# Taking a D-skip off TensorE: x loaded into the output tile, multiplied by D and added on VectorE

## The chip, the cores and the metric

The kernel runs on one core of one Trainium2 chip. The metric is the device time of one launch in microseconds (us). The time before is 201.72 us, the median of three runs (201.47 to 202.68). A faster kernel is one whose time is over 2% lower.

A core has five engines that matter here. TensorE multiplies matrices into PSUM. VectorE and ScalarE move results from PSUM to SBUF and do elementwise work. GpSimd does some elementwise work, and SyncE issues most transfers. In this kernel each engine gets its instructions in the order of one fixed list. The DMA engines move data beside them. "Span" is the time from the first to the last instruction in the trace, and the device time is some 2 to 3 us longer. "Granted clock" is the share of full speed that TensorE was given.

## The reference, cut to what matters

Two halves with 640 columns each are computed and put side by side.

```python
def _A_ref(x, Lambda_re, Lambda_im, B_re, B_im, C_re, C_im, log_dt, Dskip):   # x: [1, 2048, 640]
    ...
    Bu = jnp.einsum("bld,pd->blp", x + 0j, B_bar)
    for t in range(L):
        h = Lam_bar[None, :] * h + Bu[:, t, :]
    ...
    y = 2.0 * jnp.einsum("blp,dp->bld", hseq, Cmat).real + x * Dskip[None, None, :]   # the D-skip
    return y

def _B_ref(q, k, v, shift_k, ssm_k, ssm_D):    # the other half: a short convolution, kv = k_shift * v,
    ...                                        # then a long convolution by FFT, times q
```

The change is about the term `x * Dskip`: one multiply and one add for each of 2048 x 640 outputs.

## The kernel before

The state-space half first multiplies x by B (40 "B products" of ten matmuls each). It then builds up states with "coefficient products" of small matrices M that are computed on chip, scans, and works down again. The last step is 16 output tiles of 128 x 640. Each tile is made in two half tiles. The D-skip is three more matmuls per half tile, x transposed times a diagonal matrix of D, accumulated into the same PSUM:

```python
def a_proj(self, r, i, due):
    ...
    for part in range(2):
        def f(e, part=part):
            ...
            for j in range(10):
                nc.tensor.matmul(P[:, part, 0:320], lhsT=hap(j), rhs=self.CT[:, j, c0:c0 + 320], start=(j == 0), stop=False)
            pieces = [(k, max(c0, 128 * k), min(c0 + 320, 128 * k + 128)) for k in range(5)]
            ...
            for q, (k, lo, hi) in enumerate(pieces):
                nc.tensor.matmul(P[:, part, lo - c0:hi - c0], lhsT=self.xT[:, k, i // 2, r, ...],
                                 rhs=self.diagD[:, k, lo - 128 * k:hi - 128 * k], start=False, stop=(q == len(pieces) - 1))
        op(f"py{part}_{r}{i}", ...)
    self.evac(f"ey_{r}{i}", 640, ...)          # PSUM to the output tile yo, on ScalarE (12) or VectorE (4)
    ...
    op(f"st_{r}{i}", ...)                      # the store
```

All engines get their instructions from one list of names, in which a letter picks the engine where there is a choice (A ScalarE, D VectorE, G GpSimd, S SyncE, numbers are buffers). A fragment:

```
... py0_21@0,1 e2h30/A e2h33/D kvs4/S e321/A py1_21 s2k23@2 ey_21/A s2h32@6 e2k23/D st_21/S ...
```

Here `e2h33/D` says that an evacuation of 1024 columns stands on VectorE at that place of its queue. The order is fixed before the run. An engine whose next instruction isn't ready waits for it, as TensorE does for 1.8 us at L909 in the waits below.

## Time and profile before

| before | value |
|---|---|
| time, span, granted clock (profiled run) | 202.26 us, 200.5 us, 1.000 |
| VectorE busy from 104 to 182 us | 67.8 of 78 us (87%) |
| TensorE idle behind the first 12 us, all waits listed | 3.8 us |
| first B product, first coefficient product, first projection | 11.9, 19.9, 104.6 us |
| last instruction of TensorE ends | 196.8 us |

The slices, the windows, the chain and the groups are shown in the prediction.

To follow TensorE I also matched its program with the trace and priced each block of matmuls with its undisturbed duration in the trace (a B product 1.077 us, a half tile 1.357 us and 0.143 us for its diagonals, and so on). The **lag** is the time at which a block starts minus the work done until then. It counts waits and slow stretches alike. Before, it is 9.9 us at the first coefficient product, 17.6 us at the first projection and 23.7 us at the end. The work is 196.8 - 23.7 = 173.1 us.

### The profile page before, as it was taken

To read this page: it belongs to the slowest core of one execution; us is meant where nothing else is said; L and a number is where in the kernel's file an instruction comes from. 1 tells how busy PE (TensorE), PEld (TensorE's weight loads), DVE (VectorE), ACT (ScalarE), POOL (GpSimd) and SP (SyncE) were. 2 spreads that over 40 slices of the span, in tenths; PEclk is the share of its full clock that TensorE was granted. 3 is DMA by queue.
4 is the path that set the end of the run, shared out by engine and by line. 5 is a ranking of instruction groups with operands and counts; after the bars stand their busy time and mean duration, and the time that the engine had idled before them with its cause. 6 is when DMAs were issued, how large, how long until landed. Compare 5 with 4: busy or idle time off the path is not lost.

```text
span 200.5 us, 8859 instructions
## 1 busy us (share of the span) xinstructions
PE 185.7 (93%) x4043; PEld 136.3 (68%) x4043; DVE 168.1 (84%) x264; ACT 148.1 (74%) x175; POOL 20.6 (10%) x35
## 2 busy tenths in 40 slices
PE   0599999979999999699999999999999999999982
PEld 0465566747777678467657777676787878788771
DVE  7899899876899999949988899788959999877540
ACT  4979998978899888389986749896967679752011
POOL 8056500700000000000000000100000010001010
PEclk9999999999999999999999999999999999999999
DMA  5999997999999999969995068509334334998985
GB/s 167 239 152 132 231 180 167 245 159 210 219 180 171 167 217 206 247 153 215 210 196 133 5 152 252 134 22 189 89 147 103 96 80 105 170 234 160 229 226 140
DMA packets 109959, 33.74 MB, mean 168 GB/s; under 512 B 107106, under 2 KB 108642, under 8 KB 109922
## 3 DMA queue, kind: packets, MB, share of 16 engines
q1 hardware_dynamic: 109668, 32.52, 83.9%
q8 instruction: 31, 0.51, 1.1%
q0 software_dynamic: 224, 0.66, 0.9%
q14 instruction: 6, 0.05, 0.1%
q10 hardware_dynamic: 30, 0.00, 0.0%
HBM read 9.19 MB, written 7.86 MB: 85 GB/s over the span
## 4 chain that ended last, share of the span: by engine, by line
PE 72%; DMA 14%; DVE 6%; ACT 3%; SPq 2%; issue 1%; POOL 0%; DVEq 0%; POOLq 0%; ACTq 0%
PE ps L806 20%; PE ps L658 17%; PE ps L909 9%; PE ps L945 8%; PE ps L231 4%; DMA s<-s 4%; PE ps L1001 4%; DMA s<-in_B_v_dram 4%; PE ps L233 4%; PE ps L1037 3%; DMA s<-in_A_x_dram 3%; DMA s<-in_B_ssm_k_dram 3%; DVE s L239 2%; PE ps L810 2%; ACT s L237 2%
## 5 line engine op out<-in xcount | busy, mean ns | idle before, releaser
L237 ACT CAST s<-ps 128x1024 bf16<-128x1024 f32 x86 | 84.1, 1018 | 16.9 <-PE ps L945 6.4
L658 PE MATMUL ps<-xT,BC 128*64 128x512 bf16 x400 | 49.1, 383 | 0.1
L806 PE MATMUL ps<-BC,hb 128*128 128x320 bf16 x240 | 36.4, 300 | 0.0
L658 PEld LDWEIGHTS <-BC 128*64 128x64 bf16 x400 | 22.3, 110 | 15.1 <-issue 0.9
L806 PEld LDWEIGHTS <-hb 128*128 128x128 bf16 x240 | 21.9, 98 | 8.7 <-issue 0.3
L968 DVE TENSOR_TENSOR s<-s,s 128x2048 bf16<-128x2048 bf16 x20 | 24.4, 1222 | 2.0 <-ACT s L237 0.7
L909 PE MATMUL ps<-R,s 64*64 64x128 bf16 x1280 | 22.5, 218 | 2.9 <-POOL s L831 1.8
L237 ACT CAST yo<-ps 128x640 bf16<-128x640 f32 x12 | 8.4, 698 | 22.7 <-PE ps L810 18.5
L909 PEld LDWEIGHTS <-s 64*64 64x64 bf16 x1280 | 18.7, 107 | 8.1 <-issue 3.7
L239 DVE CAST s<-ps 128x1024 bf16<-128x1024 f32 x14 | 17.0, 1220 | 8.3 <-PE ps L909 2.7
L945 PE MATMUL ps<-s,Wre 128*64 128x128 bf16 x320 | 21.4, 221 | 0.0
L763 DVE TENSOR_TENSOR hb<-ps,hb 128x512 bf16<-128x512 f32 x30 | 19.1, 684 | 2.8 <-PE ps L231 1.6
L945 PE MATMUL ps<-s,Wim 128*64 128x128 bf16 x320 | 21.2, 219 | 0.0
L945 PEld LDWEIGHTS <-Wre 128*64 128x64 bf16 x320 | 18.2, 110 | 2.5 <-issue 0.5
L884 DVE TENSOR_TENSOR s<-s,s 128x2048 bf16<-128x2048 bf16 x15 | 18.3, 1222 | 1.0 <-ACT s L876 0.7
L945 PEld LDWEIGHTS <-Wim 128*64 128x64 bf16 x320 | 18.1, 110 | 1.1
L1044 DVE TENSOR_TENSOR s<-ps,s 128x1024 bf16<-128x1024 f32 x10 | 11.8, 1216 | 4.1 <-PE ps L1037 3.9
L237 ACT CAST hb<-ps 128x768 bf16<-128x768 f32 x17 | 13.7, 808 | 1.1 <-PE ps L658 1.1
L968 DVE TENSOR_TENSOR s<-s 128x1024 bf16<-128x1024 bf16 x20 | 13.8, 688 | 0.3
L231 PE MATMUL ps<-hb,M 128*64 128x256 bf16 (+1 forms) x136 | 13.3, 296 | 0.0
L1037 PE MATMUL ps<-Ct,s 128*64 128x64 bf16 x640 | 11.6, 196 | 0.8 <-DMA s<-s 0.7
L1037 PEld LDWEIGHTS <-s 128*64 128x64 bf16 x640 | 11.1, 113 | 1.9 <-DMA s<-s 0.9
(157 smaller groups left out, 261.4 us busy)
## 6 DMA issues: line engine op xcount, KB each, us to landing
s<-in_B_ssm_k_dram SPq DMA_DIRECT2D x5, 512.0 KB, 4.7
kvd<-s SPq DMA_DIRECT2D x5, 512.0 KB, 4.4
s<-kvd SPq DMA_DIRECT2D x5, 512.0 KB, 5.6
s<-in_B_q_dram SPq DMA_DIRECT2D x5, 512.0 KB, 4.4
out_dram<-s SPq DMA_DIRECT2D x5, 512.0 KB, 5.1
out_dram<-yo SPq DMA_DIRECT2D x12, 160.0 KB, 2.8
s<-in_A_x_dram SPq DMA_DIRECT2D x2, 640.0 KB, 4.8
out_dram<-yo POOLq DMA_DIRECT2D x4, 160.0 KB, 3.4
```

Source lines behind the costliest of these rows:

```text
L231: self.nc.tensor.matmul(out[h], lhsT=lhsT[:, h], rhs=rhs, **k)
L237: self.nc.scalar.copy(out=out, in_=in_)
L239: self.eng[e].tensor_copy(out=out, in_=in_)
L658: nc.tensor.matmul(P[64 * ri:64 * ri + 64, b, :], lhsT=self.BT[:, k, ri, 64 * j:64 * j + 64], rhs=self.xT[:, k, hf, 2 * b:2 * b + 2, :].re ...
L763: v.tensor_tensor(out=hv(r), in0=self.P(p2)[:, 0, :].rearrange("p (h m) -> p h m", h=2), in1=hv(r), op=ALU.add)
L806: nc.tensor.matmul(P[:, part, 0:320], lhsT=hap(j), rhs=self.CT[:, j, c0:c0 + 320], start=(j == 0), stop=False)
L884: op(f"ca{j}{G}{h}", {"DVE": dve_tt(W_)}, lambda e, c=c, tt=tt: v.tensor_tensor(out=c(), in0=c(), in1=tt(), op=ALU.add), r=[f"tm{G}{h}"], ...
L909: nc.tensor.matmul(P[64 * ri:64 * ri + 64, r, 128 * b4:128 * b4 + 128], lhsT=d[64 * r:64 * r + 64, 4 * qd + b4, a0, :], rhs=self.R[64 * r: ...
L945: nc.tensor.matmul(P[64 * pi:64 * pi + 64, ri, 128 * k4:128 * k4 + 128], lhsT=W[:, kp, pi, :], rhs=A[:, kp + 16 * pi, :], start=True, stop ...
L968: v.tensor_tensor(out=o, in0=a, in1=b, op=op_)
L1037: nc.tensor.matmul(P[64 * ah:64 * ah + 64, b // 8, 64 * (b % 8):64 * (b % 8) + 64], lhsT=Z[:, 16 * h + b, 64 * ri:64 * ri + 64], rhs=self. ...
L1044: v.tensor_tensor(out=o, in0=self.P(pt)[:].rearrange("p s (b a c) -> p a (s b) c", b=8, a=16), in1=o, op=ALU.mult)
```

## The change

Its intent: relieve TensorE of the 96 diagonal matmuls by having the x rows loaded straight into the output tile, multiplied by a broadcast D on VectorE, and added as the tile is evacuated. VectorE is relieved in turn by handing other evacuations to ScalarE. B is loaded in smaller pieces so that the first product can start early, and TensorE multiplies zeros while it waits for data. The core of the diff:

```diff
@@ a_proj
-                    nc.tensor.matmul(P[:, part, 0:320], ..., start=(j == 0), stop=False)
-                pieces = ...                                  # three diagonal matmuls
-                ...
+                    nc.tensor.matmul(P[:, part, 0:320], ..., start=(j == 0), stop=(j == 9))
-        self.evac(f"ey_{r}{i}", 640, ...)
+        op(f"xl_{r}{i}", ... dma_start(out=self.yo[yo.slot][:], in_=self.x2[r0:r0 + 2033:16, :]) ...)
+        op(f"xm_{r}{i}", ... nc.vector.tensor_tensor(out=yo, in0=yo, in1=self.Db[:], op=ALU.mult) ...)
+        op(f"ey_{r}{i}", ... nc.vector.tensor_tensor(out=yo, in0=self.P(pt)[:, :, 0:320], in1=yo, op=ALU.add) ...)
@@ a_B
-        for h in range(2):
+        for h, (lo, n) in enumerate(((0, 128), (128, 192), (320, 320))):      # B in three pieces of rows
@@ setup
+            for _ in range(8):
+                nc.tensor.matmul(self.P(warm)[:, 0, :], lhsT=self.xT[...], rhs=self.xT[...], start=True, stop=True)   # zeros
@@ build
-        self.yo = [T([128, D], bf16, f"yo{i}") for i in range(2)]
+        self.yo = [T([128, D], bf16, f"yo{i}") for i in range(4)]
@@ ORDER
-... (the whole list)
+... (a new list: every engine's order changes)
```

Cut are some scratch tiles that now share memory with others, and the list, which is new from its first word on.

## The prediction

> **What bounds the kernel now.** I read the page first (engine shares, the slices), then the chain that ended last in order of time, then the groups with shapes kept apart, then a table of windows. The slices come first:
>
> ```profile
> PE   0599999979999999699999999999999999999982
> DVE  7899899876899999949988899788959999877540
> ACT  4979998978899888389986749896967679752011
> DMA  5999997999999999969995068509334334998985
> ```
>
> TensorE is at nine tenths or more nearly everywhere, VectorE is close behind it, and the DMA engines are full up to slice 21 and then half empty. The windows (window in us; length; busy us and count of TensorE matmuls, weight loads, VectorE, ScalarE, GpSimd; clock; DMA share; GB/s) show the same by stage:
>
> ```profile
> 0.00:9.68 9.68, 2.66 (x23) 2.12 (x24) 8.11 (x31) 6.87 (x10) 4.62 (x17) 1.00 0.86 200
> 69.00:104.77 35.77, 33.73 (x780) 23.81 (x769) 31.32 (x59) 28.91 (x38) 0.52 (x2) 1.00 1.07 206
> 104.77:150.00 45.23, 45.10 (x955) 33.94 (x952) 39.04 (x50) 35.14 (x34) 0.82 (x2) 1.00 0.49 127
> 150.00:182.00 32.00, 31.95 (x794) 26.06 (x790) 28.38 (x30) 23.70 (x26) 1.08 (x2) 1.00 0.66 137
> ```
>
> From 104.77 us (first output projection) TensorE has no idle time until 182 us, and VectorE is busy 67.4 of those 77.2 us (87%). Busy matmul time is overlapped time, so I take TensorE's real price from the chain, which lists start, length and piece. The projection of one half tile (ten matmuls of 320 columns, then three diagonal ones for the D-skip) and the end:
>
> ```profile
> 106.27 1.36 PE ps L806 x10
> 107.63 0.14 PE ps L810 x3
> ...
> 182.68 8.76 DMA s<-s
> 191.48 2.21 PE ps L1037 x128
> 193.70 1.46 PE ps L806 x10
> 195.30 1.36 PE ps L806 x10
> 196.66 0.15 PE ps L810 x3
> 196.84 0.69 ACT yo L237
> ```
>
> So 1.36 us is the projection and 0.14 us the D-skip. The end is: last DMA transpose of the other half of the model, two inverse stages (2.21 us), the last tile's two projections, evacuation, store.
>
> The groups carry the durations that the sums below use:
>
> ```profile
> L806 PE MATMUL ps<-BC,hb 128*128 128x320 bf16 x240 | 36.4, 300 | 0.0
> L810 PE MATMUL ps<-diagD,xT 128*128 128x128 bf16 x64 | 8.8, 219 | 0.0
> L810 PE MATMUL ps<-diagD,xT 128*128 128x64 bf16 x32 | 6.2, 193 | 0.0
> L237 ACT CAST yo<-ps 128x640 bf16<-128x640 f32 x12 | 8.4, 698 | 22.7 <-PE ps L810 18.5
> L709 DVE TENSOR_TENSOR cw<-sinT,ps 128x640 bf16<-128x640 bf16 x4 | 3.3, 816 | 2.2 <-PE ps L231 2.2
> L707 DVE TENSOR_TENSOR cw<-cosT,cw 128x640 bf16<-128x640 bf16 x2 | 1.0, 482 | 0.0
> ```
>
> The 15.0 us shown for the diagonal matmuls (8.8 + 6.2) is latency of overlapping instructions; at 0.14 us per three it is 4.5 us of TensorE. L709 is a tensor_tensor of 640 columns that reads PSUM, as the new evacuation will be: 816 ns. L707 is one of 640 bf16 columns in SBUF, as x times D will be: 482 ns.
>
> **What the Trainium skill says.** "Perfetto Trace Analysis", § Identifying the Most-Contended Engine: matmul busy time doesn't tell how close TensorE is to its limit, occupancy does so for VectorE and ScalarE. The trace agrees: 15.0 us of shown diagonal time is 4.5 us in the chain. "VectorE: DVE Perf Modes", § The perf-mode tier table: tensor_tensor runs at twice the base rate on bf16 in SBUF and at the base rate with a PSUM operand; 482 against 816 ns for 640 columns agrees. "TensorE: Matmul & The Clock Gate", § Part 1: the clock is half after an idle stretch and is released after about 3.4 us of activity. The page of this kernel prints a full clock in all slices, but the first 40 transposes have weight loads of 143 ns where the same 128x128 load takes 98 ns later, and 20 of them take 2.31 us (115 ns each), so I believe the slow start.
>
> **The change part by part.**
> 1. TensorE loses 96 diagonal matmuls: 32 half tiles x 0.143 us = 4.6 us. They stand in the stage in which TensorE has no idle time, so this is worth its full size unless another engine takes over.
> 2. Evacuation: 12 ScalarE copies (12 x 0.70 = 8.4 us) and 4 VectorE copies (4 x 0.82 = 3.3 us) go; 16 PSUM adds (16 x 0.82 = 13.1 us) and 16 products (16 x 0.485 = 7.8 us) come to VectorE, and the making of the diagonal (1.25 us) goes: +16.3 us on VectorE alone. The new order pays for this by handing work to ScalarE: seven of the fourteen 1024-column evacuations (7 x 1.22 = 8.5 us), two of the three 768-column ones (1.9 us), two more conv scalings (1.5 us on VectorE, 4.0 on ScalarE), three small tap adds to GpSimd (1.1 us), with 1.3 us coming back from others. Net about +4.5 us on VectorE, +3 us on ScalarE.
> 3. Loads: 16 x-tile loads of 160 KB and the broadcast D row. Thirteen of the sixteen come when the DMA engines are half idle, and with four output tiles instead of two they are issued well ahead. I take nothing for them.
> 4. Start. Real work starts now at 11.93 us, when the first B transposes have landed and the second x half has been transposed (that load was issued at 4.19 us and landed at 9.64). The changed order issues the second x load directly after the first and the small ones, and B's first piece is 128 rows. By the landing of what the first product needs, 1.31 MB of x and 0.57 MB of B (448 rows x 1280 B, because one 192-row piece goes first) have moved instead of 1.31 + 0.82 MB. Before, 2.13 MB took from about 1.75 to about 11.7 us, 213 GB/s; 1.88 MB at that rate land at about 10.5 us. The eight products of zeros stand in front of the last transposes of x and should fit before that. Gain 1.4 us. The first 70 products took 8.10 us instead of 35 x 0.2155 = 7.54; with a warm clock 0.5 us more. Together about 2 us.
>
> To see who bounds the middle I added up each engine's instructions along the program's order, with the durations of the groups. From the first projection to the issue of the last DMA transpose: before, TensorE 75.4, VectorE 72.3, ScalarE 60.8 us, and it took 77.9 us (104.77 to 182.68), 97% of TensorE. After: TensorE 68.6, VectorE 72.8, ScalarE 64.9 us. VectorE becomes the longest. At the same 97% it takes 72.8 / 0.97 = 75 us: 3 us gained of TensorE's 6.8 us. Ahead of the projections the sums hardly differ (TensorE 87.4 before, 87.9 after; ScalarE 88.4 and 88.8), so that stage gains only the start plus perhaps 0.5 us of its waits (one of 1.76 us at 82 us for a tap add behind a load, one of 1.11 at 43 us). Behind the last transpose: two inverse stages and one tile as before, 0.3 us less for the diagonals, 0.12 us more for the evacuation.
>
> Sum: 2.5 (start and first stages) + 3 (projections) + 0 (end) = 5.5 us. 201.7 - 5.5 = 196.2 us.
>
> **Rivals.**
> - *TensorE stays the bound everywhere.* Then 4.6 + 2 = 6.6 us or a little more, 194.5 to 195. For it: the new order balances the three engines within 1 us at most cuts up to the last projections (at the twelfth half-pair TensorE 152.8, VectorE 152.9, ScalarE 152.7 us), so nobody must wait long if the order fits the chip. Against it: no slack on any of three engines.
> - *VectorE becomes a hard bound with stalls of its own.* It now takes part in every projection tile, in the same strict order as the products and scans; one late input holds the evacuation, which holds PSUM, which holds TensorE. With 92% use instead of 97% the projection stage takes 79 us, a loss of 1 us, and the time is about 200. Against it: four output tiles, and x times D is done ahead of the projection.
> - *Load queue.* SyncE issues the new x loads between blocking waits: its DMA transposes hold it for 5 us each, and a store that waits for its evacuation holds the next load behind it. If x is late, VectorE waits for it in order. This would cost 1 to 3 us: 197 to 199.
> - *Start doesn't move.* If the coefficient chain (first used by the product at 19.93 us) or the later B pieces bind instead, the start gives 0.5 us: 197.7.
>
> **Range and chances.** The gain of 5.5 us has three uncertain terms: the start (0.5 to 3), the projection stage (-1 to 5), the waits of the early stage (-1 to 2). I take 193.2 to 199.8 us for 8 in 10. Faster by over 2% needs under 197.7 us, 1.5 us above the point: 0.68. Within 2%: 0.29. Slower by over 2% would need a new stall of some 10 us: 0.03.
>
> **What would show it.** Right: no diagonal matmuls, first B product at about 10.5 us; first projection near 102 us; VectorE above 92% busy between it and the last transpose, with TensorE now showing short waits for VectorE; last transpose issued near 177 us; the tail of 18 us as before. Wrong: VectorE idle in that stage before its products with the x tiles, waiting for their load (the queue rival); TensorE idle for microseconds in the first 20 us (the start); or TensorE still without gaps and a time under 194 us.

## More of the kernel before

The FFT half has five groups. For each it convolves k, multiplies by v, writes the result to memory, reads it back in another layout, and runs forward stages (`s1`, `s2`), products, and inverse stages (`i2`, `i1`). Its loads and its write and read-back all go through SyncE:

```python
op(f"kvs{G}", {"SP": 0.4, ...}, ... dma_start(out=d[:], in_=...) ...)            # write
op(f"kvl{G}", {"SP": 0.4, ...}, ... dma_start(out=..., in_=d.rearrange(...)) ...)  # read back
```

One more view is needed for the comparison, the waits of TensorE. Each line gives what waited, for whom, how long in total, how many times, and the longest:

```profile
PE ps L909 <- POOL s L831: 1.8, 1, 1.8
PE ps L909 <- ACT s L237: 1.1, 1, 1.1
PE ps L1037 <- DMA s<-s: 0.7, 1, 0.7
PE ps L786 <- ACT s L237: 0.2, 1, 0.2
```

Left out is the wait for the first loads of x. What to see: there is no line "issue", which is the name for a wait for which the profile shows no releaser. TensorE, once started, has four short waits in 190 us.

## The result, and the profile after

The changed kernel is slower: 208.88 us median of six runs (206.76 to 209.33) against 202.08 us for the kernel before in the same rounds (201.17 to 203.77). The ratio is 1.0305, with a 95% interval of 1.0238 to 1.0371. Ratios here are the mean time of one kernel's fast runs over that of the other's fast runs of the same rounds, so not quite the ratio of the medians quoted. All outputs are right.

The slices of the changed kernel, each digit a busy share in tenths of a fortieth of the span:

```profile
PE   0899999796999999899999999999999999999972
DVE  7589989486699999959998996989988988998761
ACT  2998997776799888548999796988897889841000
DMA  5999987999999999999993539996942994199975
```

Counted from 0, TensorE has dents at slices 7, 9 and 16 (before: 8 and 16), and VectorE is thin from 7 to 10 as it was around 8 and 9 before. The second half looks as full as before. The slices alone don't show where 3% went. The stages after the first projection (length; busy us and count of TensorE matmuls, weight loads, VectorE, ScalarE, GpSimd; clock; DMA share; GB/s):

```profile
109.37:150.00 40.63, 39.69 (x850) 27.80 (x848) 37.06 (x50) 34.47 (x29) 1.26 (x3) 1.00 0.79 184
150.00:182.00 32.00, 32.00 (x726) 24.52 (x722) 29.21 (x36) 26.82 (x29) 0.55 (x1) 1.00 0.56 117
```

VectorE is at 91% here (87% before); the prediction named above 92%. But TensorE reads full although it has less to do. The new instructions are in the groups (form and count, then busy us and mean ns, then idle before):

```profile
L818 DVE TENSOR_TENSOR yo<-ps,yo 128x640 bf16<-128x640 f32 x16 | 13.1, 823 | 4.2 <-PE ps L810 3.6
L816 DVE TENSOR_TENSOR yo<-yo,Db 128x640 bf16<-128x640 bf16 x16 | 7.5, 483 | 0.2 <-DMA yo<-in_A_x_dram 0.2
L340 PE MATMUL ps<-xT 128*128 128x512 bf16 x8 | 3.3, 593 | 0.0
```

Their sizes are those of the prediction, and the products wait 0.2 us in all for their loads, so the load queue doesn't hold VectorE. The chain that ended last (start, length, piece):

```profile
10.13 3.13 PE ps L340 x8
...
13.48 7.67 PE ps L662 x70
...
32.44 6.13 DMA s<-in_B_v_dram
...
40.23 5.45 DMA kvd<-s
...
45.69 5.60 DMA s<-kvd
51.34 1.53 PE ps L913 x96
...
184.27 9.62 DMA s<-s
193.89 0.04 issue
193.93 2.18 PE ps L1041 x126
196.12 1.24 issue
197.36 0.22 PE ps L1041 x2
197.58 2.84 PE ps L810 x20
```

Three things are new. The zeros (L340) stand on the path at the start and take 3.13 us, and the first B product starts at 13.4 us, 1.5 us later than before. Then the chain runs for 19 us through loads of the FFT half: v of group 0 is issued at 32.44 us (25.45 before), the first convolution result is written and read back, and TensorE resumes at 51.34 us. And two matmuls from the end of an inverse stage, TensorE waits 1.24 us for nothing that the profile shows. Its waits (the one for the first loads is left out):

```profile
PE ps L913 <- POOL s L835: 2.4, 2, 1.3
PE ps L913 <- DMA s<-kvd: 2.1, 1, 2.1
PE ps L1041 <- issue: 1.7, 2, 1.2
PE ps L913 <- issue: 0.3, 1, 0.3
PE ps L235 <- DVE Qb L753: 0.2, 1, 0.2
```

In the whole run TensorE waits for VectorE once, for 0.2 us.

To see where the time went, cut both profiled runs at the points that the prediction names:

| stretch | before, us | predicted, us | after, us |
|---|---|---|---|
| start to the first projection | 104.6 | about 102 | 109.2 |
| first projection to the issue of the last DMA transpose | 78.1 | 75 | 75.1 |
| last DMA transpose to the end of the span | 17.8 | as before | 19.8 |
| device time outside the span | 1.8 | no term | 3.1 |

(The prediction counted from 104.77 us, the place of the first projection in the chain, and so had 77.9 us for the second stretch before.) **The stage of the projections gained the 3 us that were forecast. The loss lies on both sides of it**: 4.6 us ahead, where a gain of 2.5 us was forecast, 2.0 us behind, and 1.3 us outside the span. Behind it, the last transpose takes 9.62 us of the chain (8.76 before) and the wait without a releaser 1.24 us. A second trace of the same program, told below as a_again, has 110.0, 75.4, 19.9 and 3.4 us. The size of the first loss is less sure: in the nine profiled kernels with the changed order the first projection comes at 107.4 to 110.9 us (median 109.2), in the eleven with the order of before at 104.6 to 108.0 us (median 106.3), so the profiled run before is the earliest of its kind.

The longer "issue" waits of all traces share one regularity. The trace also has the queues that fetch instructions. The Trainium skill, "Runtime: NRT & Kernel Launch", § Instruction fetch mechanics, says that they come in blocks of 16 KB, 256 instructions. One queue has 31 packets of 16 KB here (30 of them within the span), 7,936 instructions by that figure, and TensorE has 7,905 matmuls and weight loads, so I take this queue for TensorE's. In this run a packet runs from 194.83 to 196.03 us, and the wait ends at 197.36, 1.33 us later. In all profiled runs together TensorE has 51 waits without a releaser of 0.3 us or more, and every one of them ends 1.2 to 1.8 us after the end of a packet of this queue. So I read these as TensorE having run out of instructions. The times argue for it strongly; no run forced it.

With the lag, the whole difference can be written down. TensorE's work fell from 173.1 to 168.7 us, as intended. Its lag at the end rose from 23.7 to 31.7 us: 196.8 - 4.4 + 8.0 = 200.4 us, where its last instruction ends. The half tiles did get cheaper by what was promised: from the start of one matmul to that of the next, the 32 half tiles take 45.9 us instead of 50.4. What was gained there was lost elsewhere.

In the seven profiled runs in which TensorE's queue fetches once more after the end of the span (the changed kernel, at 206.6 us, and six variants of it), time minus span is 2.9 to 3.4 us. In the 13 others it is 1.8 to 2.3 us. So a late fetch may be what the end waits for. That too is read from the times only.

### The profile page after: what moved, and what is told of

The parts are those of the page before. It is cut to its first block, busy times and chain, and to the rows that moved or that the text cites. A ratio compares the mean times of both kernels' runs of the same rounds, so it can differ in the third digit from the quotient of the medians.

```text
span 204.1 us, 8701 instructions
## 1 busy us (share of the span) xinstructions
PE 187.2 (92%) x3952; PEld 130.9 (64%) x3953; DVE 172.6 (85%) x275; ACT 151.1 (74%) x172; POOL 22.2 (11%) x39
## 4 chain that ended last, share of the span: by engine, by line
PE 63%; DMA 19%; DVE 11%; issue 2%; ACT 2%; SPq 1%; POOL 0%; ACTq 0%; POOLq 0%; DVEq 0%
PE ps L810 19%; PE ps L662 12%; PE ps L913 7%; PE ps L949 7%; DMA s<-s 5%; PE ps L1005 4%; PE ps L235 4%; PE ps L1041 3%; DMA s<-in_B_ssm_k_dram 3%; PE ps L233 3%; DMA s<-in_A_x_dram 3%; DMA s<-in_B_v_dram 3%; DMA s<-kvd 3%; DMA kvd<-s 3%; DVE M L436 2%
## 5 line engine op out<-in xcount | busy, mean ns | idle before, releaser
L239 ACT CAST s<-ps 128x1024 bf16<-128x1024 f32 x93 | 90.7, 1018 | 21.2 <-PE ps L913 10.2
L662 PE MATMUL ps<-xT,BC 128*64 128x512 bf16 x400 | 48.6, 380 | 0.0
L810 PE MATMUL ps<-BC,hb 128*128 128x320 bf16 x240 | 35.7, 300 | 0.0
L913 PE MATMUL ps<-R,s 64*64 64x128 bf16 x1280 | 24.0, 218 | 4.8 <-POOL s L835 2.4
L913 PEld LDWEIGHTS <-s 64*64 64x64 bf16 x1280 | 19.3, 106 | 13.0 <-issue 7.3
L972 DVE TENSOR_TENSOR s<-s,s 128x2048 bf16<-128x2048 bf16 x20 | 24.5, 1223 | 0.7
L767 DVE TENSOR_TENSOR hb<-ps,hb 128x512 bf16<-128x512 f32 x30 | 19.6, 687 | 3.3 <-PE ps L235 2.4
L949 PE MATMUL ps<-s,Wim 128*64 128x128 bf16 x320 | 20.9, 219 | 0.0
L239 ACT CAST hb<-ps 128x768 bf16<-128x768 f32 x19 | 14.9, 804 | 3.8 <-PE ps L662 3.6
L880 ACT ACTIVATE s<-s,sk 128x2048 bf16<-128x2048 bf16 x8 | 15.8, 2002 | 1.3 <-DVE s L888 1.3
L1048 DVE TENSOR_TENSOR s<-ps,s 128x1024 bf16<-128x1024 f32 x10 | 11.9, 1220 | 5.7 <-PE ps L1041 3.3
L818 DVE TENSOR_TENSOR yo<-ps,yo 128x640 bf16<-128x640 f32 x16 | 13.1, 823 | 4.2 <-PE ps L810 3.6
L972 DVE TENSOR_TENSOR s<-s 128x1024 bf16<-128x1024 bf16 x20 | 13.8, 688 | 0.3
```

Of the source, the lines that this page charges most:

```text
L239: self.nc.scalar.copy(out=out, in_=in_)
L662: nc.tensor.matmul(P[64 * ri:64 * ri + 64, b, :], lhsT=self.BT[:, k, ri, 64 * j:64 * j + 64], rhs=self.xT[:, k, hf, 2 * b:2 * b + 2, :].re ...
L767: v.tensor_tensor(out=hv(r), in0=self.P(p2)[:, 0, :].rearrange("p (h m) -> p h m", h=2), in1=hv(r), op=ALU.add)
L818: op(f"ey_{r}{i}", {"DVE": dve_p(640)}, lambda e: nc.vector.tensor_tensor(out=self.yo[yo.slot][:].rearrange("p (b n) -> p b n", b=2), in0= ...
L880: nc.scalar.activation(out=out, in_=k(j), func=ACT.Copy, scale=self.sk[:, G, j:j + 1])
L913: nc.tensor.matmul(P[64 * ri:64 * ri + 64, r, 128 * b4:128 * b4 + 128], lhsT=d[64 * r:64 * r + 64, 4 * qd + b4, a0, :], rhs=self.R[64 * r: ...
```

## The experiments

My theory after the first look: the loss is not in the D-skip's own instructions but in the new order, early loads first. The rivals: VectorE is the bound; the x loads cost; the zeros and pieces cost. Each run is compared with the kernel before of its own rounds. Runs in a slow state (low clock or over 1.5% above the kernel's fastest) are left out of ratios.

### The changed kernel's order, with and without the D-skip

**a_again**: the changed kernel once more, unchanged, to stand beside the variants.

> The changed kernel unchanged, for comparison within the same rounds. All theories: 3% slower than before, as when it was first measured; its spans vary with the clock record and with TensorE's waits without a releaser.

Measured: 208.65 us (205.96 to 210.41), ratio 1.0219 (1.0129 to 1.0308). This is lower than the first 1.0305, within both intervals. So I take the loss as 2.2 to 3.1%.

**a_diag**: its order, but the D-skip back on TensorE and all 16 output evacuations on ScalarE (12 of them in the kernel before).

```diff
-xl_.. xm_..            (16 loads, 16 products, 16 adds on VectorE)
+diagD, three diagonal matmuls per half tile; ey_../A
```

> The changed kernel with the D-skip back on TensorE: 96 diagonal matmuls, evacuation by a ScalarE copy, no x tiles loaded, no product with D, everything else in the changed order (zeros, pieces of B, loads). Theory V (VectorE took over in the projection stage; the D-skip's move costs what it saves): the time stays within 1 us of the changed kernel or falls by up to 3 us, with TensorE's excess over its work from 100 us on back at about 6 us instead of 11. Rival P (TensorE is the bound and the move is a gain that is hidden by losses elsewhere): the time rises by 3 to 4.6 us.

Measured: 208.69 us (207.92 to 209.74), ratio 1.0237 (1.0159 to 1.0314). In this order the time is the same, within the intervals, whether TensorE or VectorE does the D-skip. That doesn't make the move worthless: the projection stage of this trace takes 78.5 us, against 75.1 and 75.4 us in the two traces of the changed kernel, but the changed kernel has 1.3 to 1.6 us more outside its span. And ScalarE is fuller here (busy 88% of the stage, 83% in the changed kernel), so the two differ in more than TensorE and VectorE.

**a_nodiag**: the same order and no D-skip at all. Its output is wrong, which doesn't matter for the time.

```diff
 # a_diag, and
-                for q, (k, lo, hi) in enumerate(pieces): nc.tensor.matmul(... diagD ...)
```

> The changed kernel's order with no D-skip at all (wrong on purpose): no diagonals, no products, no x loads, evacuations on ScalarE. Beside it stand the changed kernel (1.022) and the same order with the D-skip on TensorE (1.024). If that order is bound by TensorE, taking the 96 diagonals away gives the 2% that it gave in the order of before: 1.00 to 1.005. If the order itself has lost the 2% in waits: 1.015 to 1.025, whatever does the D-skip.

Measured: 207.83 us (207.18 to 209.79), ratio 1.0316 (1.0241 to 1.0391). Even with nobody doing the D-skip this kernel is 3% slower than the kernel before, so the D-skip's own instructions can't be the whole cause. It is not a clean test of the order: all 16 output evacuations stand on ScalarE, on top of those that the change had handed to it, ScalarE is busy 91% of the projection stage (83% in the changed kernel), and TensorE waits for it there. No run was made with some of them on VectorE. Free of this is the stretch ahead of the projections: the first comes at 107.4 us, 2.8 us later than before. The waits of TensorE show where part of the 4.5 us less of work went:

```profile
PE ps L1042 <- issue: 2.5, 2, 2.0
PE ps L232 <- POOL M L435: 2.1, 2, 1.4
PE ps L914 <- DMA s<-kvd: 1.9, 1, 1.9
PE ps L914 <- ACT yo L238: 1.0, 1, 1.0
```

They are late instructions at the end, coefficient sets that GpSimd makes too late, the read-back, and an output evacuation on ScalarE. Its lag at the end is 32.2 us, against 30.5 us in a_diag.

### The kernel before, without the D-skip on TensorE

**b_nodiag**: only the diagonal matmuls taken out. Its output is wrong, which doesn't matter for the time.

```diff
-                for q, (k, lo, hi) in enumerate(pieces): nc.tensor.matmul(... diagD ...)
```

> The kernel before without its 96 diagonal matmuls, so that the D-skip is missing: its output is wrong on purpose. It measures what taking the matmuls away is worth when nothing has to be done in their place. Theory V and P both: 3.5 to 4.6 us faster than before (197.5 to 198.6). If another engine or a transfer is just behind TensorE in the projection stage, less than 2 us.

Measured: 199.97 us (199.24 to 200.82) against 203.78, ratio 0.9807 (0.9735 to 0.9879): 1.9%, or 3.9 us. The first term of my sum (4.6 us) lies within the interval, in the order of before.

**b_dskip**: the order of before, D-skip on VectorE as in the change (loads, products and adds placed by hand, nothing else moved).

```diff
-ey_21/A
+xm_21 (ahead of py0_21) ... ey_21 (add, VectorE);  xl_.. on SyncE two tiles ahead
```

> The order of the kernel before with only the D-skip moved: x tiles loaded (four output tiles), product and adding evacuation on VectorE, B in two halves as before, no zeros, no other operation moved between engines. Theory V: +16 us on VectorE in a stage in which it was 87% busy, so the 4.5 us saved on TensorE are lost again and more: 2 to 6 us slower than before. Rival P: 2 to 4 us faster than before. Theory O (the loss of the change lies in the early order): as fast as before or faster.

Measured: 211.91 us (207.16 to 213.57); three of four runs were slow. The profiled run, a slow one, had VectorE at 97.6% from 104 to 150 us. Its runs settle no size.

**b_dskip_act**: the same, and seven 1024-column evacuations handed from VectorE to ScalarE, as the change does.

```diff
-e2h33/D e2k23/D e2k31/D e1h41/D e2h41/D e322/D e332/D
+e2h33/A e2k23/A e2k31/A e1h41/A e2h41/A e322/A e332/A
```

> The order of the kernel before, D-skip on VectorE as in the last experiment with it, and seven 1024-column evacuations handed from VectorE to ScalarE to pay for it (8.5 us off VectorE, 7.1 us onto ScalarE), as the change did. Theory V: VectorE in the projection stage falls from 97% busy to about 90% and the time lies between before plus 1 and before plus 5 us. If the early order alone made the changed kernel slow, this one is 2 to 4 us faster than before.

Measured: 209.2 us (208.38 to 215.59), ratio 1.0287 (1.0217 to 1.0357). So from 0.981 to 1.029, 4.9%, is the price of having the D-skip on VectorE in the order of before. That is more than twice what TensorE saves. In its trace (a fast run) the projection stage takes 82.2 us, against 74.9 us in b_nodiag and 75.1 us in the changed kernel: the new list does solve this stage, which the old one with the move done by hand doesn't. Five more runs took this apart; all of them have no D-skip. Their outputs are wrong, which doesn't matter for the times. Four of them (b_ne, b_nl, b_nel, b_ne0) also have the shared scratch tiles and the four output tiles of the change. The profiled runs of b_ne, b_nl, b_nel and b_mv are slow ones.

**b_ne**: all 16 output evacuations on VectorE as plain copies, and the seven handed to ScalarE.

```diff
-ey_21/A ... e2h33/D ...
+ey_21/D ... e2h33/A ...
```

> Ladder between the kernel before without its diagonals (ratio 0.981) and the kernel before with the D-skip on VectorE (1.029), step 1: no D-skip at all (output wrong on purpose), but all 16 output evacuations on VectorE instead of 4, as plain copies from PSUM, with the same seven 1024-column evacuations moved to ScalarE. If the evacuations' place on VectorE and its order is what costs, this alone brings back most of the 9 us: ratio about 1.01 to 1.02. If it is the loads or the products, ratio stays at 0.98 to 0.99.

Measured: 208.91 us (206.28 to 212.12), ratio 1.0239 (1.0137 to 1.0341). With no load and no product, nearly the whole 4.9% is there.

**b_nl**: evacuations as before, but the 16 x loads are issued (each evacuation overwrites its loaded tile).

```diff
+xl_32/S xl_03/S ...
```

> Ladder, other branch: no D-skip at all (wrong on purpose), evacuations on ScalarE and VectorE as before, but the 16 x-tile loads and the broadcast D row are issued at the places they have in the kernel with the D-skip on VectorE; the evacuation writes over the loaded tile, so it must wait for the load. If the loads cost by themselves (SyncE's queue, DMA traffic, late instruction fetches): ratio 0.995 to 1.01, against 0.981 without them. If they are free, as I predicted: 0.98.

Measured: 203.28 us (200.81 to 206.43), ratio 0.9934 (0.9876 to 0.9992). The loads, shared tiles and further output tiles together stand 1.3% over b_nodiag; the intervals just meet, so I call it likely.

**b_nel**: both, so that only the products and the second operand of the add are missing.

```diff
+xl_32/S ... ; ey_../D ; the seven /A
```

> Both steps of the ladder, so that only the 16 products with D (7.8 us of VectorE) and the add's second operand are missing from the kernel with the D-skip on VectorE (1.029). If the costs add up, its ratio over 0.981 is the product of the two single steps. If the products are what fills VectorE, this stays under 1.0 and the last step to 1.029 is the largest.

Measured: 208.92 us (206.51 to 211.23), ratio 1.024 (1.0152 to 1.0328). The loads add nothing to b_ne, and the products can have at most the 0.5% that is left to 1.0287, which is within the intervals.

**b_mv**: b_nodiag and nothing but the seven evacuations moved to ScalarE.

```diff
-e2h33/D e2k23/D e2k31/D e1h41/D e2h41/D e322/D e332/D
+e2h33/A e2k23/A e2k31/A e1h41/A e2h41/A e322/A e332/A
```

> The kernel before without diagonals (wrong on purpose, 0.981), and the seven 1024-column evacuations moved from VectorE to ScalarE; the output evacuations stay on ScalarE (12) and VectorE (4). If handing those seven to ScalarE is what made the 16-on-VectorE kernel slow (1.024), this is slow too: 1.01 to 1.03. If the output evacuations on VectorE are what costs, this stays at 0.98 to 0.99.

Measured: 206.68 us (204.01 to 209.23) against 201.8, ratio 1.0154 (1.0065 to 1.0243), from two fast runs of four. This is 3.5% above b_nodiag, with the same matmuls, the same loads and less work on VectorE. The profiled run is one of the two slow ones (207.08 us), so the sizes that follow are of that run and don't explain the ratio. The waits of TensorE, and the end of its chain:

```profile
PE ps L806 <- issue: 2.7, 1, 2.7
PE ps L940 <- ACT s L237: 1.7, 4, 0.7
PE ps L940 <- issue: 1.3, 1, 1.3
...
PE ps L1032 <- issue: 0.9, 1, 0.9
```

```profile
194.17 0.51 PE ps L806 x3
194.68 2.71 issue
197.39 3.81 PE ps L806 x17
```

TensorE waits four times for ScalarE at L940, all after 104 us, where b_nodiag has no wait for ScalarE at all. At 194.68 us it seems to run out of instructions (a packet ends at 196.09, 1.30 us ahead of the wait's end). The 17 matmuls behind that take 3.81 us instead of 17 x 0.136 = 2.31 us, because the granted clock falls to 0.59 in the 2 us from 198 us on. So a wait of 2.7 us cost 4.2 us. Lag from first projection to end: 13.8 us, against 7.3 us in b_nodiag.

**b_ne0**: all 16 output evacuations on VectorE, the seven left where they were.

```diff
-ey_21/A
+ey_21/D
```

> The kernel before without a D-skip (wrong on purpose), all 16 output evacuations on VectorE, and none of the seven evacuations moved to ScalarE: VectorE has 9.8 us more than in the kernel before without diagonals. If VectorE's amount of work is the bound of the projection stage, this is slower than the same with the seven moved (1.024): 1.03 to 1.05. If the seven moved ones were the cost: 0.99 to 1.01.

Measured: 207.43 us (205.69 to 208.41), ratio 1.0258 (1.019 to 1.0325), 4.6% above b_nodiag. Its profiled run is a fast one. TensorE's waits from 100 us on:

```profile
PE ps L800 <- issue: 2.2, 1, 2.2
PE ps L231 <- DVE hb L757: 1.2, 2, 0.9
PE ps L233 <- DVE hb L757: 1.2, 1, 1.2
PE ps L934 <- DVE s L239: 0.5, 1, 0.5
PE ps L1026 <- issue: 0.5, 1, 0.5
```

The projection stage takes 78.1 us, 3.2 more than in b_nodiag, of which some 2.9 us are waits for VectorE that b_nodiag doesn't have. The stretch behind it takes 21.1 us, 3.3 more; in it lies the wait of 2.2 us without a releaser, behind which the granted clock is 0.50 from 197 to 200 us. So about half of this loss is a hand-over that came late, and about half is at the end. The slow trace of b_mv divides alike: 2.5 us more in the stage, with 2.3 us of waits for ScalarE, and 3.9 us more behind it.

Both moves cost by themselves, and together (b_ne) no more than either: neither of the two theories that I had set against each other is right alone. What the two have in common is that work was moved in a queue whose order had been fitted to its neighbours. That this is the reason is an inference from the waits.

### The start

**a_nowarm**: the changed kernel without the eight products of zeros.

```diff
-wz/D ... warm@2
```

> The changed kernel without the eight products of zeros (and the clearing of their operand), nothing else. Theory Z (the zeros stand in TensorE's way: 3.1 us between the second half's second and third transposes while B's first piece has landed at about 10 us): the first B product starts at 10.5 us or a little later instead of 13.48, and the time falls by 1 to 3 us. Rival O (the start is given back, because the order of the loads binds TensorE by 51 us in any case): the first product moves forward but the stall at 49 to 51 us, which waits for the first conv group, grows by as much and the time changes by less than 0.5 us.

Measured: 209.88 us (207.46 to 214.73), ratio 1.0199 (1.009 to 1.0308), two of four runs slow. The first B product starts at 11.3 us instead of 13.4, and the first coefficient product at 20.1 us. Not distinguishable from a_again.

**b_pieces**: the kernel before with B in the three pieces and the product of the first piece first.

```diff
-B00 ... B01 ... B10 ... B11 ;  dn0_2_0@4 ... dn0_0_0@6
+B00 B01 ... B10 B11 ... B20 ... B21 ;  dn0_0_0@4 ... dn0_2_0@6
```

> The kernel before with B in three pieces per half of the complex matrix and the product that needs only the first piece put first; nothing else. Theory S (the start is bound by the coefficient chain: the first product that uses the coefficients stands at 19.9 to 20.1 us in five of six profiles, wherever the first B product starts): first B product some 0.5 to 1.5 us earlier, first coefficient product unmoved at 19.9, time within 0.5% of before. Rival (the prediction's step on the start): 1 to 2 us faster.

Measured: 204.0 us (202.2 to 205.62), ratio 1.0024 (0.9955 to 1.0094). The first coefficient product starts at 20.0 us. In all eleven profiled kernels with the order of before, the first B product starts anywhere from 10.6 to 11.9 us and the first coefficient product at 19.9 or 20.0: it waits for its coefficients, not for B. In the changed order it comes 7.6 to 7.8 us behind the first B product (8.8 us in a_nowarm), at 19.2 to 21.0 us.

### The early loads

**a_v0**: the transpose of v of group 0 issued after the fifth of the eight x transposes.

```diff
-s1h03@4,4 e1_8_0/A set_1_1/D dn1_7_0 e1h03/A v0@6
+x131 v0@6 ...
```

> The changed kernel with one load moved: the first v transpose is issued after the fifth of the eight second-half x transposes, as the kernel before has it, instead of after the eighth. Theory O (early loads): v lands some 3.5 us earlier (about 35 instead of 38.6 us), the write and read-back of the first conv group move with it, and TensorE's wait of 2.05 us at 49 to 51 us goes; 1.5 to 3.5 us faster than the changed kernel of the same rounds. Rival (what is lost there is lost again later, or another load binds): within 0.7 us.

Measured: 206.82 us (205.03 to 207.35), ratio 1.0168 (1.0099 to 1.0237), beside 1.0219 of a_again in the same rounds. TensorE's wait for the read-back, which was to go, is still there with 2.5 us.

**a_v0k**: a_v0, and the first convolution's write ahead of the load of k of group 1.

```diff
-kz1/G@3 k1 ... kvs0/S
+kvs0/S kz1/G@3 k1
```

> The changed kernel with two places of SyncE's queue put back: the first v transpose after the fifth second-half x transpose (as in the last experiment), and the write of the first conv group ahead of the second k transpose, which holds SyncE until ScalarE has freed its buffer. Theory O (head of the line): the write is issued at about 37.8 us instead of 40, the read-back lands at about 48.5 instead of 51.3, TensorE's wait of 2.5 us there goes, and the kernel is 2 to 3 us faster than with the v load alone (ratio to before about 1.005). Rival: the wait moves to another load, ratio 1.015 to 1.02 as before.

Measured: 206.39 us (205.09 to 207.52), ratio 1.0156 (1.0102 to 1.0211). The write was issued at 37.63 us instead of 40.23, but the read-back only at 44.23, since the transpose of v of group 1, which waits for a buffer, stood before it on SyncE.

**a_fix**: a_v0k, and the read-back ahead of that transpose.

```diff
-kvs0/S ... v1@0 ... kvl0/S@5
+kvs0/S ... kvl0/S@5 v1@0
```

> The changed kernel with the order of its early loads mended completely: v0's transpose after the fifth x transpose, the first convolution write ahead of k1, and its read-back ahead of v1's transpose. Theory (early order costs part of the gap): read-back lands at about 48.5 us instead of 51.3, TensorE's 2.05 us wait at 49.3 falls under 0.5 us, ratio 1.008 to 1.014. Rival (the stage is limited by the three engines' sums and any wait reappears later): 1.016 to 1.022 as without the edit.

Measured: 205.63 us (205.25 to 205.92), ratio 1.0154 (1.0117 to 1.0191). The wait for the read-back is gone from TensorE's list. The lag at the first FFT stage that needs it is 12.6 us instead of 15.9, so 3.3 us were won there. But at the first projection it is 20.4 instead of 21.7 us, and the time is 0.65% better than that of a_again, 1.3 us, which is within the intervals. Both theories are half right: mending the early order seems to give 1.3 us, and most of what is mended comes back later.

### The product on GpSimd

**a_gps**: the changed kernel, product with D on GpSimd.

```diff
-op(f"xm_{r}{i}", {"DVE": ...}, lambda e: nc.vector.tensor_tensor(
+op(f"xm_{r}{i}", {"POOL": 1.7}, lambda e: self.eng[e].tensor_tensor(
```

> The changed kernel with the 16 products of x and D on GpSimd instead of VectorE, in the same places of the order: 7.5 us off VectorE, some 26 us onto the idle GpSimd. Theory V (VectorE's load in the projection stage causes TensorE's small waits): 1 to 3 us faster than the changed kernel (ratio to before 1.007 to 1.017), excess of TensorE over its work from the first projection to the end down from 10 us. Rival: GpSimd and VectorE disturb each other (the set products on VectorE took 1299 ns instead of 969 while GpSimd made others), or VectorE is not what TensorE waits for: no change or slower.

Measured: 213.48 us (212.22 to 214.65), ratio 1.0503 (1.044 to 1.0565). The 7.5 us were taken off VectorE, and it got slower:

```profile
L972 DVE TENSOR_TENSOR s<-s,s 128x2048 bf16<-128x2048 bf16 x20 | 29.7, 1486 | 1.0 <-PE ps L1005 0.4
L816 POOL TENSOR_TENSOR yo<-yo,Db 128x640 bf16<-128x640 bf16 x16 | 25.5, 1604 | 55.9 <-DMA yo<-in_A_x_dram 33.5 <-DMA Db<-in_A_Dskip_dram 22.4
```

A product takes GpSimd 1604 ns instead of 483, and VectorE's products of 2048 columns (L972) take 1486 ns in the mean instead of 1223. The twenty of them alone lose 5.2 us. The Trainium skill, "SBUF — State Buffer", § Who interferes with whom, says that a VectorE instruction with two SBUF inputs contends with a GpSimd one that reads SBUF. This trace agrees.

**b_gps**: the same product on GpSimd in the order of b_dskip_act.

```diff
 # b_dskip_act, and
-xm_.. on VectorE
+xm_.. on GpSimd, one tile ahead; all stores on SyncE
```

> The order of the kernel before with the D-skip off TensorE, the product of x and D on GpSimd one projection ahead, the adding evacuation on VectorE, seven evacuations handed to ScalarE, all stores of this half from SyncE. VectorE then has about as much to do as before. Theory V: 4 to 6 us faster than the same with the products on VectorE, so between before minus 3 us and before plus 1 us. Rival as for the last one: as slow as with the products on VectorE (ratio 1.03).

Measured: 213.24 us (206.84 to 217.12), four of six runs slow; ratio of the fast ones 1.0192 (1.0116 to 1.0269), of two runs. It settles little.

### Over all runs

Two columns of the traces go with the times. TensorE's waits without a releaser, summed over the profiled run, and the mean granted clock of all runs of a kernel (the clock record shows windows of 3.41 us at half clock; one of them lowers the mean by 3.41 x 0.5 / 205 = 0.008):

| kernel | ratio | waits without releaser, us | mean clock |
|---|---|---|---|
| before | 1 | 0.0 | 0.997 to 0.999 |
| b_pieces (diagonals kept) | 1.002 | 0.6 | 0.997 |
| a_diag (diagonals kept) | 1.024 | 0.3 | 0.994 |
| b_nodiag | 0.981 | 2.1 | 1.000 |
| b_mv (profiled run slow) | 1.015 | 5.2 | 0.990 |
| b_ne0 | 1.026 | 4.2 | 0.987 |
| b_ne (profiled run slow) | 1.024 | 5.5 | 0.991 |
| b_dskip_act | 1.029 | 3.8 | 0.991 |
| changed kernel | 1.031 | 2.0 | 0.996 |
| a_nodiag | 1.032 | 3.2 | 0.994 |
| a_fix | 1.015 | 3.0 | 0.998 |

The three kernels that keep the diagonals have at most 0.6 us of such waits. All 17 profiled kernels without them, eleven of them in fast runs, have 1.6 us or more. Why, no run tells. Some of these waits lie at 49 us, where TensorE's list is still the same in before and b_nodiag, so the number of instructions can't be the whole reason.

No variant with a right output beats the kernel before, b_pieces being equal to it.

## Why the prediction was wrong, point by point

**What held.** Step 1, the diagonals: 32 x 0.143 = 4.6 us were promised, and taking them out of the kernel before gave 1.9%, 3.9 us. The durations of step 2 were right: the adds took 823 ns and the products 483 ns. The rival of the load queue fell: VectorE waited 0.2 us in all for x tiles.

The term that looked most daring held too: "At the same 97% it takes 72.8 / 0.97 = 75 us". The projection stage took 75.1 us, and 75.4 us in a_again, as short as in b_nodiag (74.9 us), where nobody does the D-skip. Its mechanism is not shown by that. VectorE was to become the longest, "with TensorE now showing short waits for VectorE", but TensorE waited for VectorE once in the run, for 0.2 us, and VectorE was busy 91.5% of the stage. What stretched TensorE's 68.6 us of work to 75 us is not known, so the agreement may be luck in part. The 97% belongs to a list and not to the engines: with the same D-skip on VectorE in the old list (b_dskip_act) the stage took 82.2 us. The rival "VectorE becomes a hard bound with stalls of its own" came nearest with its 200 us, but by its number alone: its stage of 79 us didn't come.

**The step that failed most: "Ahead of the projections the sums hardly differ ... so that stage gains only the start plus perhaps 0.5 us".** The first projection was forecast near 102 us and came at 109.2: 4.6 us lost where 2.5 us were to be gained. By the lag, which leaves out that slightly more work stands in front, it is 4.1 us (21.7 us against 17.6 us). I had compared amounts of work there and not the order of the loads, though the comparison of the lists lay before me: v of group 0 stood behind eight transposes on SyncE. What the runs showed in place of the step: TensorE's waits in this stretch for other engines and for the read-back of the convolution sum to 4.7 us (3.1 before), and the first coefficient product comes 1.1 us later. In a_fix, with the loads put back in order, the first projection comes 1.3 us earlier. The rest isn't attributed one by one; the traces of a_again and a_nodiag name coefficient sets on GpSimd and tap adds.

**"The tail of 18 us as before"** failed as well, by 2.0 us: 19.8 us here, 19.5 to 20.9 us in all nine profiled kernels of the changed order. On the chain of this run 1.24 us are the wait without a releaser and 0.9 us the longer last transpose. Why that is longer isn't known.

**Step 4, the start.** "First B product at about 10.5 us", and 2 us gained: it was 13.4 us in the profiled run, where the zeros stood in front of the last transposes and took 3.13 us. It was 11.4 us in a_again, the same program, and yet the first projection came no earlier there (110.0 us). More to the point, hardly any gain is to be had. In the order of before, the first coefficient product stays at 19.9 or 20.0 us whenever the first B product starts, and in the changed order the earliest of nine profiled kernels has it at 19.2 us. This was my fourth rival, and in the order of before it was right: the coefficient chain binds.

**Step 3, the loads.** "I take nothing for them": b_nl puts 1.3% on loads, shared tiles and further output tiles together in the order of before. Beside the moved evacuations it adds nothing.

**The moves tried alone.** The sums say nothing against b_mv and b_ne0. b_mv has no more work than b_nodiag on TensorE, 8.5 us less on VectorE and some 7.1 us more on ScalarE, which by my sums had over 14 us to spare (60.8 against 75.4 us). It loses 3.5%. b_ne0 adds 9.8 us to VectorE and loses 4.6%. A sum over a stage doesn't see that a hand-over comes late, nor what happens at the end.

**What I did not think of.** TensorE's waits without a releaser on the last stretches (1.7 us in the changed kernel), half-clock windows (three of the six runs have a clock of 0.991 or 0.992 and spans of 205.3 to 206.8 us, against 204.1 and 204.5 of the two with a full clock; the sixth, at 0.998, has 205.9), and 1.2 us outside the span in the mean of the six runs. The prediction's sum had no term for any of them. A new stall of some 10 us, which it asked for before a slower kernel, isn't in the trace: behind the first loads, TensorE's longest wait is 2.1 us. The loss came in pieces.

**The sum in the end.** In the profiled run 4.6 us were lost ahead of the projections, 3.0 gained in their stage and 2.0 lost behind it, so the span is 3.6 us longer. The mean span of the six runs, those of low clock among them, is 1.3 us above that run's (205.45 against 204.1 us), and 1.2 us more pass outside the span. That is 6.1 of the 6.2 us between the means (208.37 against 202.21 us).

**What stays open.** Which of the many changes of the list cost how much ahead of the first projection and at the end; what makes TensorE's instructions late; and whether a list made anew for the D-skip on VectorE, with the early loads as in before, would win the 1.9%. The changed kernel's own list was made anew, and did so in the projection stage only. With the first stretch and the tail of before and its own middle, 104.6 + 75.1 + 17.8 = 197.5 us of span, an estimate that no run tested.

## What to carry to other kernels

Cut a result at the points that the prediction named before looking for the cause: here the stage that the change was about gained what was forecast, and the loss lay ahead of it and behind it. When several engines are above 85% in a fixed order, moving work to an engine with slack can cost more than it saves, so try the move alone on the chip, with the saved work left out even at the price of a wrong output, before building the rest. Compare the two lists queue by queue for what is issued later, not only the sums of work. And judge a gain at the start by the first instruction that needs everything, not by the first that runs.

## What the Trainium skill lacked or had wrong

- "Runtime: NRT & Kernel Launch", § Instruction fetch mechanics, calls the cost of crossing a 16 KB border mostly hidden. Here TensorE waited for no releaser up to 2.2 us in one place in a fast run (b_ne0) and 3.5 us in a slow one (b_gps), and each of 51 such waits ended 1.2 to 1.8 us after the end of a 16 KB packet. The sums were 0.0 us in the kernel before and 1.6 to 5.9 us in the 17 kernels without the diagonals.
- "TensorE: Matmul & The Clock Gate", § Part 1, names an idle window of about 3.4 us behind which the clock is half, and for one other kernel frequent short idles; it gives no size for a single shorter wait. Here single shorter waits within a busy program led to half clock: 2.2 us in b_ne0 (clock 0.50 from 197 to 200 us) and 2.7 us in b_mv, where 17 matmuls took 3.81 instead of 2.31 us.
- No page relates the time outside the span to a late fetch of instructions: time minus span was 2.9 to 3.4 us in the seven profiled runs in which TensorE's queue fetched after the end, and 1.8 to 2.3 us in the 13 others.
- "Perfetto Trace Analysis", § Identifying the Most-Contended Engine, advises to optimize the engine with the highest occupancy first. It doesn't say that this can fail under a fitted order: taking 8.5 us from VectorE, busy 91% of the projection stage in b_nodiag, and giving the work to ScalarE made the kernel 3.5% slower (b_mv).
